# A written sequence for each engine, shared bursts for head pairs, and a last step of plain products

## The chip, the cores and the metric

The kernel runs on one core of a Trainium2 chip. A core has a matrix engine (PE; its weight loads are shown apart as PEld), a vector engine (DVE), a scalar engine with function tables (ACT), a general engine (POOL) and a queue for transfers (SP). Each works through its own instructions in the order in which they were written and waits where it needs another's result. The metric is device microseconds of one execution: 678.94 us, median of 3 runs (678.92 to 679.0).

## The reference

Windowed attention with 8 global tokens and a bias by distance, and behind it a dense layer of 512 to 2048 to 512 with g = h cos(h):

```python
scores = scale * np.matmul(q, k.transpose(0, 1, 3, 2))         # 4 x 8 heads x 768 x 768
is_local = (rel >= 0) & (rel < n_local)                        # n_local 96, n_global 8
scores = np.where(is_global | is_local, scores + bias, -1e9)
a = np.exp(scores - scores.max(-1, keepdims=True)); a /= a.sum(-1, keepdims=True) + 1e-9
x = np.matmul(a, v)                                            # 3072 tokens x 512
h = x @ w_in; out = (h * np.cos(h)) @ w_out
```

## The kernel before

**Attention.** The sequences are cut into 11 parts (`OPEN`, `BLOCKS`): the first batch into two of four blocks of 96 tokens, the others into two of three blocks and one of two. A unit is one part and one pair of heads, 44 in all. For a unit PE writes scores (line 663 or 667), DVE puts masks in and takes the extreme (685, 694), ACT takes exponents with their sums (719), DVE forms reciprocals (727, 730), POOL multiplies (`norm`, 743 and 748), PE turns the result over (847), ACT and DVE bring it to SBUF as `pv`, and a *burst* (890) multiplies it with the values into a bank `px`. The burst's matmuls use 64 columns of the array for each of the two heads, all other large products use 128. `plan_x` splits the bank into a high and a low part (`xmem`).

**Dense layer.** 104 steps (`self.seq`). A step multiplies one or two groups of 128 hidden columns (`m1`, line 973, 12 or 24 matmuls), ACT and DVE form g (991, 994, 997, 1030), g is split into `gh` and `gl`, and after a lag the second product follows. Parts 0 to 2 use plain products (986). From part 3 on (`FAST`) a step of 2 x 2 blocks uses seven products in place of eight (1191), after Strassen and Winograd: DVE or POOL form sums of blocks of g (`sf`, `sh`, `sl`), sums of the weights were stored before (`plan_combined`) and are streamed in (`ws`). Each product is three matmuls of 128x256, high times high, high times low and low times high. Banks A to D collect them over the eight steps of a part, and at a part's end nine additions (`plan_outputs`) give two output tiles; the last part has a version of its own (`plan_last`, 1231). Parts 0 to 2 have a simple copy (`plan_store`, 1262).

**What sets the order.** `Plan` knows each operation with its engines, guessed costs, predecessors and tile classes. `Plan.run` (154) is a list schedule: at each moment a free engine takes, of the operations whose inputs are there by its own clock, the one with the earliest due time, and an operation that several engines may do goes to the one that would end it first, weighted by `HURRY` and `WEIGHT`. Tiles and banks are given out on the way. `emit` writes the result, and until 45 us of the plan's clock it puts matmuls on zeros (`idle`, 1518) into gaps on PE. Only two of the eight banks serve scores, turned tiles and bursts in the later parts (`att`). Two units share a burst where a part has two blocks or its number is in `MERGE`:

```python
MERGE = tuple(range(11, 11))                                   # line 67: none
both = nb == 2 or n in MERGE                                   # plan_values
cls = "part" if keep else "wu" if m < FAST else "oo"           # plan_store
```

Of the kernel before, what the change touches and what calls it, by code (L numbers as in the profile page):

```python
# [10 lines left out]
F32 = mybir.dt.float32  # L11
F32R = mybir.dt.float32r
# [9 lines left out]
P = 128  # L22
# [44 lines left out]
MERGE = tuple(range(11, 11))  # L67
DIFFER = tuple(range(4, 11))
BEFORE = {0: 4000, 1: 2500, 2: 25000}
# [4 lines left out]
FILL_TO, FILL_REST, FILL_EACH, FILL_FIRST, FILL_COLD = 45000, 150, 250, 10, 7000  # L74


class Slot:


    def __init__(self, cls, make):  # L80
        self.cls, self.make = cls, make
        self.users = 0
        self.at = None
        self._tile = None
# [21 lines left out]
class Plan:  # L106
# [7 lines left out]
    AHEAD = 2500  # L114
    SWITCH = 170
    DRAIN = 113
    DEFER = 4000

    def __init__(self, places, free):
        self.ops = []  # L120
        self.places = {c: list(v) for c, v in places.items()}
        self.busy = {}
        self.free = dict(free)
        self.port = 0
        self.mode = None
        self.last = {}

    def drained(self, o, e):

        last = self.last.get(e)  # L130
        return e in (DVE, POOL) and last is not None and (last in o.after or o.apart or last.apart)

    def op(self, engines, emit, after=(), uses=(), due=None, table=None, extra=0, port=False, mode=None):
        o = Op(engines, emit, after, list(uses), due, table, extra, port, mode)
        for a in o.after:
# [6 lines left out]
    def dues(self):  # L142
        late = 10**9
        for o in reversed(self.ops):
            d = late if o.due is None else o.due
            for t in o.then:
                d = min(d, t.due - min(t.engines.values()) - self.WAIT[next(iter(o.engines))] - o.extra)
            o.due = d

    def place(self, u, t):  # L150

        return min(self.places[u.cls], key=lambda p: self.busy.get(p, 0))

    def run(self):

        self.dues()
        for i, o in enumerate(self.ops):
            o.key = (o.due - min(o.engines.values()), i)
        ready = {e: [] for e in self.free}
        coming = []  # L160
        for o in self.ops:
            if o.left == 0:
                for e in o.engines:
                    ready[e].append(o)
        table = "exp"
        out = []
        dma = 0
        t = 0
        inf = 10**12
        todo = len(self.ops)  # L170
        import heapq

        heap = sorted(set(self.free.values()))
        while todo:
            assert heap, [(o.engines, o.key) for e in ready for o in ready[e]][:20]
            t = heapq.heappop(heap)
            while heap and heap[0] == t:
                heapq.heappop(heap)
            again = True
            while again:  # L180
                again = False
                for e, f in self.free.items():
                    if f > t:
                        continue
                    if e == SP and dma - t > self.AHEAD:
                        heapq.heappush(heap, dma - self.AHEAD)
                        continue
                    best = None
                    held = self.port > t
                    holds = lambda o, x: x == POOL or (x == DVE and o.port)  # L190
                    rank = None
                    for o in ready[e]:
                        if o.ready > t:
                            continue
                        key = o.key
                        if self.drained(o, e):
                            key = (key[0] + self.DEFER * (self.last[e] in o.after), key[1])
                        if rank is not None and key >= rank:
                            continue
                        if held and holds(o, e):  # L200
                            continue
                        if len(o.engines) > 1:
                            wait = lambda x: max(t, self.free[x], self.port if holds(o, x) else 0) - t
                            cost = lambda x: wait(x) + o.engines[x] * (HURRY if t < HURRY_TO else WEIGHT)[x]
                            if any(cost(x) < cost(e) for x in o.engines if x != e):
                                continue
                        taken, ok = set(), True
                        for u in o.uses:
                            if u.at is None:
                                p = next(  # L210
                                    (p for p in self.places[u.cls] if self.busy.get(p, 0) <= t and p not in taken),
                                    None,
                                )
                                if p is None:
                                    ok = False
                                    break
                                taken.add(p)
                        if ok:
                            best, rank = o, key
                    if best is None:  # L220
                        continue
                    o = best
                    if e == ACT and o.table and table and o.table != table:
                        same = [x for x in ready[e] if x.table == table and x.ready <= t]
                        if table == "exp" and same:
                            o = min(same, key=lambda x: x.key)
                    for u in o.uses:
                        if u.at is None:
                            u.at, u.begin = self.place(u, t), t
                            self.busy[u.at] = inf  # L230
                    for x in o.engines:
                        ready[x].remove(o)
                    d = o.engines[e]
                    if self.drained(o, e):
                        d += max(0, self.DRAIN - (t - f))
                    self.last[e] = o
                    if e == ACT and o.table and o.table != table:
                        d += self.TABLE
                        table = o.table
                    if e == PE:  # L240
                        if o.mode != self.mode:
                            d += self.SWITCH
                        self.mode = o.mode
                    o.start, o.engine = t, e
                    end = t + d
                    if holds(o, e):
                        self.port = end
                    self.free[e] = end
                    heapq.heappush(heap, end)
                    if e == SP:  # L250
                        dma = max(end + 300, dma) + o.extra
                        end = dma + 1400
                    out.append(o)
                    todo -= 1
                    for u in o.uses:
                        u.users -= 1
                        u.end = max(getattr(u, "end", 0), end + self.WAIT[e] + (SLACK // 2 if u.cls == "att" else 0))
                        if u.users == 0:
                            self.busy[u.at] = u.end
                            heapq.heappush(heap, u.end)  # L260
                    for n in o.then:
                        n.left -= 1
                        n.ready = max(n.ready, end + (self.WAIT[e] + n.slack * (2 if e == POOL else 1) if list(n.engines) != [e] else 0))
                        if n.left == 0:
                            for x in n.engines:
                                ready[x].append(n)
                            heapq.heappush(heap, max(t, n.ready))
                    again = True
        self.length = max(self.free.values())
        return out  # L270


class Net:
# [143 lines left out]
    def plan_weight(self, src, out, at, place, n, due):  # L417

        nc, p = self.nc, self.plan
# [58 lines left out]
    def plan_combined(self, q):  # L478
# [56 lines left out]
        def keep(e):  # L535
            nc.sync.dma_start(self.store(q, 4), f32(self.wo[f, 1]))

        p.op({SP: 470}, keep, done[1], [b], extra=870, due=due)

    def store(self, q, k):  # L540
        if (q, k) not in self.stored:
# [1053 lines left out]
```

## Time and profile before

| | |
|---|---|
| median of 3 runs | 678.94 us |
| span of the profiled execution | 676.7 us |
| outside the span, against the median | 2.2 us |
| PE busy | 663.8 us, 98% of the span |
| DVE, ACT, POOL busy | 554.6, 508.7, 391.0 us |
| useful matmuls end | 669.9 us |
| last output transfer issued | 671.4 us |

The profiled execution's own time is its span and what lies around it; the table sets its span beside the median of the runs. PE's busy time counts zero matmuls and slow changes between kinds of matmul as work, so 98% doesn't mean that nothing is to be had; where the starts of matmuls lie apart tells more. The granted clock of PE stays at its upper level from the first microseconds to the end of the matmuls.

### The profile page before, as it was taken

How to read it: one execution, taken by the hardware profiler on the slowest of the kernel's cores; microseconds unless marked ns; L12 is line 12 of the kernel's file. 1: busy time of each engine (PE TensorE's matmuls, PEld its weight loads, DVE VectorE, ACT ScalarE, POOL GpSimd, SP SyncE). 2: the span in 40 equal slices, each digit the busy share in tenths (PEclk: the TensorE clock that was granted, in tenths of full speed). 3: DMA queues.
4: the chain of work that ended last, by engine and by line, in shares of the span. 5: the costliest groups of instructions: out<-in, count | busy, mean ns of one | idle time of the engine just before them, and what ended most of it. 6: DMA issues, size and time to landing. Idle time of an engine off the chain costs nothing. (4 is left out here: it accounts for less than half of the span.)

```text
span 676.7 us, 17496 instructions
## 1 busy us (share of the span) xinstructions
PE 663.8 (98%) x5810; PEld 626.7 (93%) x5810; DVE 554.6 (82%) x1726; ACT 508.7 (75%) x1253; POOL 391.0 (58%) x576
## 2 busy tenths in 40 slices
PE   8999999999999999999999999999999999999995
PEld 4769999999999998999999999999999999999995
DVE  7999898978898897777778888797878898887664
ACT  7999997579776785866778878676787788684432
POOL 5896544437457553467866776736876768532201
PEclk9999999999999999999999999999999999999999
DMA  8999200044546665877887867787687777665664
GB/s 279 336 321 380 80 1 1 22 159 121 163 139 194 221 183 174 239 220 203 244 240 207 249 213 231 245 239 232 210 240 219 235 228 235 199 224 187 191 226 150
DMA packets 86291, 136.69 MB, mean 202 GB/s; under 512 B 9904, under 2 KB 33968, under 8 KB 86192
## 3 DMA queue, kind: packets, MB, share of 16 engines
q1 hardware_dynamic: 86048, 135.23, 64.7%
q8 instruction: 48, 0.79, 0.5%
q14 instruction: 51, 0.42, 0.2%
q10 hardware_dynamic: 144, 0.26, 0.1%
HBM read 118.67 MB, written 16.78 MB: 200 GB/s over the span
## 5 line engine op out<-in xcount | busy, mean ns | idle before, releaser
L973 PE MATMUL bank<-xmem,w 128*128 128x256 f32 (+1 forms) x2112 | 344.4, 295 | 0.1
L973 PEld LDWEIGHTS bank<-xmem,w 128*128 128x128 f32 x2112 | 294.1, 189 | 7.7 <-issue 0.9
L719 ACT ACTIVATE tt<-tt,st 96x104 f32<-96x104 f32 (+1 forms) x256 | 94.6, 371 | 7.2 <-DVE st L694 6.5
L997 ACT ACTIVATE rr<-rr,half_pi 128x512 f32<-128x512 f32 (+1 forms) x104 | 71.6, 691 | 23.3 <-DVE rr L994 22.1
L986 PE MATMUL bank<-w,gh 128*128 128x256 f32 (+1 forms) x384 | 88.3, 320 | 0.0
L991 ACT ACTIVATE rr<-bank 128x512 int32<-128x512 f32 (+1 forms) x104 | 57.9, 558 | 30.9 <-PE bank L973 29.1
L1191 PE MATMUL bank<-ws,sh 128*128 128x256 f32 x384 | 75.8, 284 | 1.3 <-DVE oo L299 1.3
L994 DVE SCALAR_TENSOR_TENSOR rr<-rr,bank 128x512 f32<-128x512 int32 (+1 forms) x104 | 66.5, 639 | 8.2 <-ACT rr L991 7.6
L784 POOL TENSOR_TENSOR qk<-raw,qk 64x304 fp32r<-64x304 f32 (+1 forms) x57 | 50.0, 880 | 28.4 <-ACT qk L297 6.9
L748 POOL TENSOR_TENSOR tt<-tt,st 96x416 f32<-96x416 f32 (+1 forms) x60 | 45.4, 764 | 35.3 <-DVE sf L1137 9.1
L986 PEld LDWEIGHTS bank<-w,gh 128*128 128x128 f32 x384 | 62.7, 188 | 1.1
L1030 DVE TENSOR_TENSOR rr<-bank,rr 128x512 f32<-128x512 f32 x72 | 49.3, 684 | 16.6 <-ACT rr L997 16.4
L986 PE MATMUL bank<-w,gl 128*128 128x256 f32 (+1 forms) x192 | 61.1, 318 | 0.0
L1191 PEld LDWEIGHTS bank<-ws,sh 128*128 128x128 f32 x384 | 58.6, 188 | 2.0 <-issue 1.4
L297 ACT CAST gh<-rr 128x384 fp32r<-128x384 f32 (+1 forms) x76 | 39.5, 520 | 25.8 <-DVE rr L1030 10.8
L694 DVE CUSTOM_DVE_ANT_0 tt<-bank,dd 96x104 f32<-96x104 f32 (+1 forms) x256 | 55.0, 256 | 2.2
L1191 PE MATMUL bank<-ws,sl 128*128 128x256 f32 x192 | 54.1, 282 | 0.1
L997 ACT ACT_TABLE_LOAD x40 | 51.3, 1283 | 0.7
L719 ACT ACT_TABLE_LOAD x39 | 50.0, 1283 | 0.7
L445 POOL TENSOR_SCALAR raw<-raw 128x512 bf16<-128x512 bf16 (+1 forms) x32 | 36.6, 1167 | 23.6 <-DVE w L466 13.2
L667 PE MATMUL bank<-qk 128*96 128x200 f32 (+1 forms) x384 | 49.1, 257 | 0.0
L1191 PE MATMUL bank<-w,gh 128*128 128x256 f32 x256 | 48.7, 282 | 0.0
(137 smaller groups left out, 1532.4 us busy)
## 6 DMA issues: line engine op xcount, KB each, us to landing
ws<-sum SPq DMA_DIRECT2D x256, 256.0 KB
raw<-in_qk_dram SPq DMA_DIRECT2D x48, 174.0 KB
raw<-in_w_in_dram SPq DMA_DIRECT2D x16, 512.0 KB
sum<-sw SPq DMA_DIRECT2D x64, 128.0 KB
raw<-in_qk_dram SPq DMA_DIRECT2D x48, 150.0 KB
raw<-in_qk_dram SPq DMA_DIRECT2D x48, 148.0 KB
out_dram<-oo SPq DMA_DIRECT2D x23, 256.0 KB
raw<-in_w_out_dram SPq DMA_DIRECT2D x16, 256.0 KB
```

What stands on the lines that cost most here:

```text
L667: nc.tensor.matmul(out, qs[:, m, q0], ks[:, k : k + w], start=m == 0, stop=m == 1)
L694: nc.vector.tensor_tensor_reduce(tt[t // 2].tile[:, t % 2, j, :w], ps.tile[:R, i * WIN : i * WIN + w], self.dd[:, v, :w], op0=ALU.add, op1 ...
L719: nc.scalar.activation(x, x, AF.Exp, bias=st.tile[:, c : c + 1], scale=-1.0, accum_out=st.tile[:, n2 + c : n2 + c + 1])
L748: self.eng(e).tensor_tensor(x, x, r.broadcast_to([R, na, SLOT]), op=ALU.mult)
L784: self.eng(e).tensor_tensor(ks[D:, k0:k1], raw.tile[D:, k0:k1], ks.bitcast(F32)[D:, k0:k1], op=ALU.subtract)
L973: self.nc.tensor.matmul(ph, self.wi[f][:, w, kk * P : (kk + 1) * P], xx[:, kk, :], start=kk == 0 and m == 0, stop=kk == self.NK - 1 and m ...
L986: self.nc.tensor.matmul(out, gg, w[:, i, :], start=start and m == 0 and h == 0, stop=stop and m == 2)
L991: self.nc.scalar.activation(r.bitcast(I32), ph, AF.Copy, scale=1.0 / TWO_PI, bias=0.25)
L994: self.nc.vector.scalar_tensor_tensor(r, r.bitcast(I32), -TWO_PI, ph, op0=ALU.mult, op1=ALU.add)
L997: self.nc.scalar.activation(r, r, AF.Sin, bias=self.half_pi)
L1030: {DVE: dve(512)}, lambda e: nc.vector.tensor_tensor(r(), h(), r(), op=ALU.mult), [o], [ph, rr],
L1191: nc.tensor.matmul(out, x, y, start=q == 0 and j == 0 and half == 0, stop=q == self.NF // 2 - 1 and j == 2 and ends)
```

## The change

A table `ORDER` gives each operation its place in one common sequence and its engine (t PE, a ACT, d DVE, g POOL, s SP). `Plan.run` follows it and only hands out tiles and banks; due times, costs and weights choose nothing any more. `MERGE` holds parts 2 to 10, so that the three-block parts too have two units in a burst. In the last step (`plan_last`) the seven products become eight plain ones of three matmuls, in two banks `att` and one `ph` that start empty; the additions for the seven steps before are done with `plan_outputs`, and what the eight products give is added to the result. Its `g` is split over its full 512 columns, its block sums go. `plan_store` of part 2 uses tiles `oo`. Two thresholds of the zero matmuls move. `COPIED`, `APART` and `BEHIND` are empty and change nothing; `low` in `step` is 0 wherever `step` runs.

```diff
-MERGE = tuple(range(11, 11))
+MERGE = tuple(range(2, 11))
-FILL_TO, FILL_REST, FILL_EACH, FILL_FIRST, FILL_COLD = 45000, 150, 250, 10, 7000
+FILL_TO, FILL_REST, FILL_EACH, FILL_FIRST, FILL_COLD = 52000, 250, 250, 10, 7000
+ORDER = {
+    "": "1s 0d 2d 3d 4d 5d 7d 8d 13d 14d",
+    "v0.0": "10s 55s",
...
 class Plan:
+    def ordered(self):
+        at, out = {}, [None] * len(self.ops)
+        names = dict(t=PE, a=ACT, d=DVE, g=POOL, s=SP)
+        for o in self.ops:
+            part = o.name.split(" ")[0]
+            i = at[part] = at.get(part, -1) + 1
+            rank = self.table(part)[i]
+            o.engine = names[rank[-1]]
+            out[int(rank[:-1])] = o
+        return out
     def run(self):
-        self.dues()
-        ready = {e: [] for e in self.free}
...
+        out = self.ordered()
+        for o in out:
+            for u in o.uses:
+                if u.at is None:
+                    free = [p for p in self.places[u.cls] if p not in held and p not in taken]
+                    u.at = min(free, key=lambda p: clear.get(p, 0))
...
 def plan_step
-        c0 = HALF if fast else 0
+        c0 = HALF if fast and s < len(self.seq) - 1 else 0
 def plan_fast
+        if s == len(self.seq) - 1:
+            self.plan_last(s, m, q, self.po, gg, g, self.before, due)
+            return
 def plan_last
+        (one, *first), (two, *second) = self.plan_outputs(m, po, last, due, False)
+        X, Y, Z = self.bank(), self.bank(), self.bank("ph")
+        plan = (
+            (1, X, lo, 0, 0, two, second), (2, X, hi, 0, 1, two, second), (3, Y, lo, 1, 0, one, first), (4, Z, hi, 1, 1, one, first),
+        )
+        for i, b, half, t, c, _, _ in plan:
+            for k in range(2):
+                def times(e, i=i, b=b, half=half, t=t, c=c, k=k):
+                    (ah, al), (bh, bl) = left(k, t), (row(c) if k else top[c])()
+                    for j, (x, y) in enumerate(((ah, bh), (ah, bl), (al, bh))):
+                        nc.tensor.matmul(half(b), x, y, start=i != 2 and k == j == 0, stop=i != 1 and k == 1 and j == 2)
+        for i, b, half, t, c, out, before in plan[1:]:
+            done[i] = p.op({DVE: 420 if i > 2 else 685}, step, [*before, ends[i]], [b, out], due=due)
 def plan_store
-            cls = "part" if keep else "wu" if m < FAST else "oo"
+            cls = "part" if keep else "wu" if m < FAST - 1 else "oo"
```

How the sequence changes is seen at three places. First PE at the first attention of part 2, before (pv, v: the burst; qk: scores of the next unit; xmem: `m1`; gh, gl: second products), two cuts from before:

```order
L973 MATMUL bank<-xmem,w 128x384 x3
L890 MATMUL bank<-pv,v 64x96 x10
L667 MATMUL bank<-qk 96x96 x2
...
L986 MATMUL bank<-w,gl 128x512
L973 MATMUL bank<-xmem,w 128x384 x3
L890 MATMUL bank<-pv,v 64x96 x10
```

and the same two units now:

```order
L1439 MATMUL bank<-ident,tt 96x96 x2
L1439 MATMUL bank<-ident,tt 104x96 x4
L1573 MATMUL bank<-xmem,w 128x384 x12
L1490 MATMUL bank<-pv,v 64x96 x20
L1255 MATMUL bank<-qk 96x96 x2
```

Two bursts of ten products have become one of twenty. Over the program PE has 38 bursts before and 26 now.

Second ACT and DVE where part 2 ends and part 3 starts (`oo<-bank` is the copy that empties a bank; the numbers tell tiles apart). ACT before, and behind the dots DVE before:

```order
L997 ACTIVATE rr_3977<-rr_3977,half_pi_112 128x512
L297 COPY oo_4019<-bank_3134 128x512
L991 ACTIVATE rr_4050<-bank_3980 128x512
...
L994 SCALAR_TENSOR_TENSOR rr_4050<-rr_4050,bank_3980 128x512
L299 COPY oo_4070<-bank_3151 128x512
L1030 TENSOR_TENSOR rr_4050<-bank_3980,rr_4050 128x512
```

and ACT now:

```order
L883 CAST gh_4029<-rr_3964 128x384
L883 COPY oo_4032<-bank_3220 128x512
L883 COPY oo_4048<-bank_3213 128x512
L1591 ACTIVATE rr_4062<-bank_3977 128x512
```

Both copies stand on ACT, one behind the other, and go to the two tiles `oo0` and `oo1`; before, both went to the one tile `late1`.

Third DVE at the end of the program, before:

```order
L1041 TENSOR_TENSOR gl<-rr,gh 128x384
L1137 TENSOR_TENSOR sf<-rr,sf 128x128
L1144 TENSOR_TENSOR sl<-sf,sh 128x512
L1242 TENSOR_TENSOR oo<-oo,bank 128x256
L1242 TENSOR_TENSOR mid<-mid,bank 128x256
L1242 TENSOR_TENSOR oo<-mid,oo 128x256
```

and now:

```order
L1630 TENSOR_TENSOR rr<-bank,rr 128x512
L885 CAST gh<-rr 128x512
L1815 TENSOR_TENSOR oo<-oo,bank 128x256 x3
L1815 TENSOR_TENSOR oo<-oo 128x256 x2
L1815 TENSOR_TENSOR oo<-oo,bank 128x256 x2
L1870 TENSOR_TENSOR oo<-oo,bank 128x512
L1870 TENSOR_TENSOR oo<-oo,bank 128x256 x2
```

The sums of blocks are gone, `gl` of the last step is POOL's last instruction, and three additions are left behind the last products.

The counts by engine change too. DVE takes from POOL 33 instructions of `norm` (9 of 96x416, 16 of 96x208, 8 of 96x192; it had none), 20 low parts of keys (64x304), 8 differences of values and most of the sums of blocks; it has 12 casts `sh` (none before), 16 more casts `gh`, and 25 sign operations on weights (8 before). `raw<-raw,steep` (the first units' queries) stands 2 times on ACT (7 before), 5 on POOL (1) and once on DVE. ACT has 8 fewer loads of a function table, PE 39 zero matmuls (48).

## Rows read from the trace of the kernel before

**Rows 1.** Page, part 1 (busy us, share, instructions) and the clock by slices.
```profile
PE 663.8 (98%) x5810; PEld 626.7 (93%) x5810; DVE 554.6 (82%) x1726; ACT 508.7 (75%) x1253; POOL 391.0 (58%) x576
...
PEclk9999999999999999999999999999999999999999
```

**Rows 2.** Windows: length, busy us by engine, clock, DMA share, GB/s.
```profile
10.00:60.00 50.00, 48.18 (x475) 35.52 (x473) 46.44 (x218) 49.71 (x169) 41.78 (x50) 1.00 0.99 340
60.00:100.00 40.00, 40.00 (x261) 37.61 (x261) 35.74 (x62) 40.00 (x90) 19.98 (x20) 1.00 0.32 108
100.00:170.00 70.00, 69.99 (x480) 65.74 (x479) 59.91 (x164) 54.60 (x128) 35.35 (x50) 1.00 0.24 75
170.00:260.00 90.00, 90.00 (x779) 84.03 (x778) 81.36 (x252) 70.68 (x172) 49.34 (x64) 1.00 0.58 183
260.00:340.00 80.00, 77.64 (x710) 75.46 (x709) 58.29 (x183) 55.08 (x131) 48.80 (x77) 1.00 0.74 215
340.00:620.00 280.00, 279.95 (x2650) 274.70 (x2650) 231.82 (x736) 213.78 (x519) 182.28 (x271) 1.00 0.75 226
```

**Rows 3.** Waits of PE from 60 us on: total us, times, longest.
```profile
PE bank L1191 <- DVE oo L299: 1.3, 1, 1.3
PE bank L847 <- DVE pv L299: 0.7, 1, 0.7
```

**Rows 4.** Zero matmuls: timeline of the first and second run of them, group by form.
```profile
1.05 3.91 PE L1518 MATMUL idle<-zeros 128*128 128x512 bf16 x10 [1.05 <-DVE zeros L307]
...
8.49 3.41 PE L1518 MATMUL idle<-zeros 128*128 128x512 bf16 x15
...
L1518 PE MATMUL idle<-zeros 128*128 128x512 bf16 x48 | 13.7, 420 | 1.1 <-DVE zeros L307 1.1
```

**Rows 5.** Timeline of PE around one burst: start us, us, instruction.
```profile
257.12 0.88 PE L973 MATMUL bank<-xmem,w 128*128 128x256 f32 x6
257.93 0.39 PE L890 MATMUL bank<-pv,v 104*64 104x96 f32 x4
258.15 0.34 PE L890 MATMUL bank<-pv,vd 96*64 96x96 f32 x4
...
259.15 0.33 PE L890 MATMUL bank<-pv,vd 96*64 96x96 f32 x4
259.42 0.97 PE L973 MATMUL bank<-xmem,w 128*128 128x256 f32 x6
```

**Rows 6.** Tile oo, 255 to 275 us: its instruction, what ended idle time.
```profile
L299 DVE COPY oo<-bank x1: 691/691/691, 269.3 to 269.3; 128x512 f32<-128x512 f32 x1
its engine sat idle before it (us, times) until:
  DMA out_dram<-oo: 1.9, 1
```

**Rows 7.** Timeline of the end.
```profile
662.06 0.40 PE L1191 MATMUL bank<-w,gh 128*128 128x256 f32 x2
...
664.44 0.69 DVE L1030 TENSOR_TENSOR rr<-bank,rr 128x512 f32<-128x512 f32 x1 [0.79 <-ACT rr L997]
...
664.53 0.40 PE L1191 MATMUL bank<-w,gh 128*128 128x256 f32 x2
...
668.12 0.19 PEld L1191 LDWEIGHTS bank<-ws,sl 128*128 128x128 f32 x1 [0.25 <-DVE sl L1144]
...
669.63 0.28 PE L1191 MATMUL bank<-ws,gl 128*128 128x256 f32 x1
...
670.76 0.42 DVE L1242 TENSOR_TENSOR oo<-mid,bank 128x256 f32<-128x256 f32 x1
...
671.41 0.38 ACTq L1258 DMA_DIRECT2D out_dram<-oo  x1
```

**Rows 8.** Groups by form: busy us, mean ns; and line 1144's spread, min/median/max.
```profile
L618 ACT ACTIVATE raw<-raw,steep 128x384 f32<-128x384 f32 x7 | 4.3, 615 | 3.7 <-POOL small L357 2.8 <-DMA raw<-in_qo_dram 0.8
...
L442 DVE TENSOR_SCALAR raw<-raw 128x512 uint16<-128x512 uint16 x8 | 6.4, 796 | 0.0
...
L1144 DVE TENSOR_TENSOR sl<-sf,sh x41: 647/693/1409, 261.5 to 667.4; 128x512 fp32r<-128x512 f32 x41
L1144 POOL TENSOR_TENSOR sl<-sf,sh x23: 1277/1289/1300, 291.8 to 637.3; 128x512 fp32r<-128x512 f32 x23
```

More of the change, by code (lines that the diff above doesn't have):

```diff
@@ new lines, with measured @@
+FILL_TO, FILL_REST, FILL_EACH, FILL_FIRST, FILL_COLD = 52000, 250, 250, 10, 7000
+def measured(e, part, name, d):
+    if e == PE:
+        if name == "score":
+            return {278: 350}.get(d, d - 2 if d < 400 else d)
+        return {"m1": {348: 358}, "times": {348: 355}, "turn": {340: 300, 170: 128}, "m2": {700: 702}}.get(name, {}).get(
+            d, d * 168 // 160 if name == "burst" else d)
+    if e == ACT:
+        if name in ("wbias", "wlow"):
+            return d + 12 if d < 400 else d - 12
+        if part[0] == "s" and name in ("op1", "op3"):
+            return d + (10 if name == "op1" else 16)
+        return d + {"khigh": 36, "qhigh": 16}.get(name, 0)
+    if e == DVE:
+        if name == "wsign":
+            return d * 83 // 100
+        return {120: 100}.get(d, d + 2 if d > 100 else d)
+    if e == POOL:
+        if name == "wsign":
+            return d * 89 // 100
+        if name == "wlow":
+            return d + (130 if d < 500 else 50)
+        if name == "wrest":
+            return d + 50 if d < 1000 else d
+        more = dict(krest=33, khigh=19, low=33, step=33, norm=15, op13=35, op15=35, wbias=40, whigh=40, queries=60)
+        return d + more.get(name, 8)
+    return d
@@ L121, in __init__ @@
         self.places = {c: list(v) for c, v in places.items()}
-        self.busy = {}
         self.free = dict(free)
[L124 to L131, printed above, removed]
-    def op(self, engines, emit, after=(), uses=(), due=None, table=None, extra=0, port=False, mode=None):
+        self.part, self.count, self.tables = "", {}, {}
+    def op(self, engines, emit, after=(), uses=(), due=None, table=None, extra=0, port=False, mode=None):
+        name = emit.__name__
+        if name == "<lambda>":
+            self.count[self.part] = self.count.get(self.part, 0) + 1
+            name = f"op{self.count[self.part]}"
+        engines = {e: measured(e, self.part, name, d) for e, d in engines.items()}
         o = Op(engines, emit, after, list(uses), due, table, extra, port, mode)
+        o.name = f"{self.part} {name}"
         for a in o.after:
@@ L140, in op @@
         return o
[L142 to L152, printed above, removed]
-    def run(self):
-        self.dues()
-        for i, o in enumerate(self.ops):
-            o.key = (o.due - min(o.engines.values()), i)
-        ready = {e: [] for e in self.free}
[L160 to L268, printed above, removed]
@@ new lines, in run @@
+    def run(self):
+        out = self.ordered()
+        port, dma, mode, table = 0, 0, None, "exp"
+        last, held, clear = {}, set(), {}
+        for o in out:
+            e = o.engine
+            taken = []
+            for u in o.uses:
+                if u.at is None:
+                    free = [p for p in self.places[u.cls] if p not in held and p not in taken]
+                    u.at = min(free, key=lambda p: clear.get(p, 0))
+                    taken.append(u.at)
+            held.update(taken)
+            t = self.free[e]
+            for a in o.after:
+                t = max(t, a.end + (self.WAIT[a.engine] if list(o.engines) != [a.engine] else 0))
+            for u in o.uses:
+                if u.begin is None:
+                    t = max(t, clear.get(u.at, 0))
+            holds = e == POOL or (e == DVE and o.port)
+            if holds:
+                t = max(t, port)
+            for u in o.uses:
+                if u.begin is None:
+                    u.begin = t
+            d = o.engines[e]
+            x = last.get(e)
+            if e in (DVE, POOL) and x is not None and (o.apart or x.apart or x in o.after):
+                d += max(0, self.DRAIN - (t - self.free[e]))
+            last[e] = o
+            if e == ACT and o.table and o.table != table:
+                d += self.TABLE
+                table = o.table
+            if e == PE:
+                if o.mode != mode:
+                    d += self.SWITCH
+                mode = o.mode
+            o.start = t
+            end = self.free[e] = t + d
+            if holds:
+                port = end
+            if e == SP:
+                dma = max(end + 300, dma) + o.extra
+                end = dma + self.LAND
+            o.end = end
+            for u in o.uses:
+                u.users -= 1
+                u.end = max(u.end, end + self.WAIT[e])
+                if u.users == 0:
+                    held.discard(u.at)
+                    clear[u.at] = u.end
@@ L489, in plan_combined @@
         one, two, tops = make(), make(), (make(), make())
-        done = [[x] + self.prev.get("sums", []) for x in done]
+        done = [[x] + self.prev.get("sums", self.joined[BEHIND:] if BEHIND else []) for x in done]
         view = lambda s: f32(s.tile)
@@ L1225, in plan_outputs @@
         v3 = p.op(ps, ad(c21, c21, bank(lo, D)), [v4, last["D"]], [D, two], due=due)
+        if not store:
+            return (one, v1, v2), (two, v3, v4)
         for z, t, after in ((one, 1, [v1, v2]), (two, 0, [v3, v4])):
@@ new lines, in plan_last @@
+        done = {}
+        for i, b, half, t, c, out, before in plan[1:]:
+            part = half if i > 2 else lambda x: x.tile
+            step = lambda e, b=b, out=out, part=part: self.eng(e).tensor_tensor(part(out), part(out), part(b), op=ALU.add)
+            done[i] = p.op({DVE: 420 if i > 2 else 685}, step, [*before, ends[i]], [b, out], due=due)
+        for x, t, after, e, queue, cs in (
+            (two, 0, [done[2]], SP, nc.sync, slice(0, 512)),
+            (one, 1, [done[3]], ACT, nc.scalar, slice(0, MW)),
+            (one, 1, [done[4]], SP, nc.sync, slice(MW, 512)),
+        ):
```

584 lines of the change are left out of this document (530 added, 54 removed), and 152 rows, old and new, of the table ORDER.

## The prediction

> **What bounds the kernel now.** I read the page's engine line and clock first: PE is busy for 98% of the span and its granted clock is full, 2.4 GHz, in every slice [rows 1]. Then the windows, for where PE is not busy: from 60 to 260 us and from 340 to 620 us it idles 0.06 us in all, from 260 to 340 us 2.36 us, and from 10 to 60 us 1.8 us [rows 2]. Then PE's waits, which name two in the middle: 1.3 us for a copy by DVE and 0.7 us for another [rows 3]. A busy PE hides two things that only the timeline shows. Of 48 zero matmuls (13.7 us busy) ten run before the first scores, in 3.9 us, and cost nothing; the other 38 take 9.8 us, 0.26 us each, and stand where PE had nothing to do [rows 4]. And a change from one kind of matmul to another is counted as work. So PE sets the time from about 60 us on, and behind it only three things can give time: fewer or cheaper PE instructions, an earlier full PE, and a shorter end. Beside PE, ACT is full from 10 to 100 us (89.7 of 90 us) and DVE is busy for 93% of 10 to 60 us [rows 2]: the ramp belongs to them.
>
> The sum is made against the profiled execution (span 676.7 us); the median of the runs lies 2.2 us above it, and I carry that over.
>
> **Shared bursts.** Twelve bursts fewer, with the same products. What a burst costs beyond its products is read at one: six matmuls start at 257.12 and the burst at 257.93, where six at the pitch of 0.118 us (21 matmuls from 662.06 to 664.53, [rows 7]) take 0.71, so 0.10 goes to the change; its eight groups lie 0.167 apart (258.15 to 259.15 is six of them) but the first took 0.22, another 0.05; and from the last group to the next `m1` are 0.27 where 0.17 would do, 0.10 [rows 5]. Together 0.25 us, times 12: -3.0 us. It is on PE in stretches where PE is full, so it counts whole if the rest keeps up. Bounds: -3.0, and 0 where PE waits instead (a rival below).
>
> **The sequence in the middle.** The 1.3 us wait is PE's first product of part 3, for a bank that DVE emptied at 269.3, and DVE had itself waited 1.9 us for an output transfer, since its copy was to go to the tile that the transfer before was still reading [rows 3, 6]. Now both copies go to two tiles and stand on ACT, behind one another. That wait goes: -1.3. The 0.7 us wait and the rest (2.36 in all from 260 to 340) come from the old order; a new order may have others, so I take half of the rest, -0.5. Sum -1.8; bounds -2.4 (all gone) and +1.5 (one wait like the 1.3 new).
>
> **The ramp.** ACT loses five multiplications of queries at 0.615 us, 3.1 us [rows 8], in a stretch in which it has 0.3 us idle out of 50 [rows 2]; up to the eighth second product the order gives it otherwise about the same work. POOL and DVE take them over, and DVE has 3.6 us idle there and gets two or three us more. The zero matmuls, which stand for the planned gaps, are 29 behind the first ten in place of 38: 9 times 0.26 is 2.3 us. So -3.1 by ACT and -2.3 by the gaps if DVE follows, about -1 if DVE's room is what counts. I take -2.0, bounds -5 (half of the 9.8 us of zeros gone) and +1. SP's transfers change places too, with DMA at 0.99 of its time from 10 to 60 us [rows 2]; none of PE's early waits is for one, and the bytes are the same, so I price that at 0 inside these bounds.
>
> **The end.** The last product of h and cos(h) ends at 664.44 + 0.69 = 665.13 [rows 7]. Behind it now come a cast of 128x512 on DVE (no row has it; about 0.4, between nothing and ACT's like at 0.6), and `gl` on POOL, for which the nearest row is POOL's subtraction of 128x512 with 1.29 [rows 8]; with 0.1 for each of two handovers, 667.0. PE's fourteen older products from 662.06, 2.47 per seven, end at 667.0 too. So the eight products start without a wait; 24 matmuls at 0.118 put the last start at 669.7, against 669.63 now [rows 7]: one product more (+0.35) is paid by the stall for `sl`, 0.25 with a weight load behind it at 668.12, which goes with the sums. What goes besides is the tail of additions: the last matmul's start lies 1.78 before the last transfer's issue at 671.41 now; then it needs its own 0.28, a handover of 0.1, one addition of 0.42 and an issue, 0.85. So -0.9. The older additions (nine) run beside the eight products. The halved last transfer may land sooner, which no row prices. Bounds -1.3 and +0.4 (POOL's `gl` 1.3 late).
>
> **Sum.** -3.0 - 1.8 - 2.0 - 0.9 = -7.7: span 669.0, with 2.2 us around it 671.2 us.
>
> **The load on DVE.** The order moves work from POOL, where an instruction takes about twice as long (1.29 against 0.69 us for `sl`, [rows 8]), to DVE. Kind by kind, with the rows' means where a row has the form, DVE gets about 20 us more up to the `m1` that runs at 169 us before; the largest kind is eight sign operations at 0.796, 6.4 us [rows 8]. This is an estimate. From 10 to 170 us DVE had 17.9 us idle [rows 2]. I take it as hidden, since the durations hold waits (`sl` on DVE takes 0.647 at the least and 1.409 at the most, [rows 8]) and POOL, with some 70 us less to do, should block less; the sum has no term for it.
> The Trainium skill, "SBUF — State Buffer", section "Who interferes with whom", says that a DVE instruction with two inputs in SBUF and a POOL instruction that reads SBUF shut each other out for a whole instruction. The spread of `sl` agrees. By that rule the added 20 us would shrink and the first rival below loses chance; without it I would give that rival more.
>
> **Rivals.**
> *DVE becomes the bound until 170 us* (slower). For it: the 20 us. It decides at how full DVE can get: PE has no idle there, so each us that DVE is short goes to PE. The other terms give -5.7 (the ramp's is lost). At 97% busy DVE has room for 155.2 - 142.1 = 13.1, is short by 6.9, and the result is +1.2, 680.1 us; at 93%, as in the ramp, it is short by 13 and the result 686. Break-even is 97.8%. Against it: shorter blocked instructions, and that some of the added work is only earlier. Chance 0.13.
> *The shared burst waits for banks.* Two units' `px` fill both `att` banks at once, and until ACT and DVE have split them neither scores nor turned tiles can be written. If PE ran dry for 0.5 us behind each of 12, 6 us of the gains go: 677.2 with everything else, 678.5 if the ramp gives 1 less. Against it: the order puts 12 or more `m1` matmuls (1.4 us) behind most shared bursts. Chance 0.08.
> *The order only trades waits.* Bursts and end stay, middle and ramp give nothing: -3.9, 675.0. Chance 0.14.
> *The ramp gives all its zeros can.* -5 in place of -2, all middle waits gone: 667.6, and below that if PE's full stretch starts even sooner. Chance 0.12.
> *The clock falls.* Fewer zero matmuls leave bare gaps. Ten took 3.91 at the start, 0.39 each, and fifteen 3.41 later, 0.23 each [rows 4]: a stretch of 4 us at the lower level, 1.2 GHz, costs some 2 us. One such stretch gives 673.2, inside my own range. Chance 0.03.
> The Trainium skill, "TensorE: Matmul & The Clock Gate", has the clock fall when the array idles; here it stays full over gaps of up to 1.3 us, so the rule changes only this small chance.
>
> **How the numbers follow.** The forecast, all four terms with their sizes within about two us, has 0.50: 668 to 675. With the rivals it makes 0.50 + 0.14 + 0.12 + 0.03 and a quarter of the bank rival faster by more than 0.2% (1.4 us, about what a measurement of this kernel can tell), 0.81; half of the bank rival and a little of the first, 0.06, within it; 0.13 slower. The range from 666 to 680 leaves out what lies past the first rival's price at 97% (about 0.09) and a ramp better than -6 (0.06).
>
> **What would show it.** Right: from 60 to 620 us PE idle below 0.5 us, 26 bursts; no wait of PE for `oo` at a part's end; the `m1` that runs at 169 us some 3 us earlier; last transfer issued within 1.0 us of the last matmul's start. Wrong: PE waits for DVE (`pv`, `xmem`, or weights) between 60 and 200 us, with DVE at 97% and more; PE idle behind shared bursts; a clock below full before 660 us.

## The result and the profile after

The changed kernel took 682.45 us (median of 4 runs, 681.92 to 683.37) against 678.93 us for the kernel before beside it: a ratio of 1.0056, 95% interval 1.0042 to 1.0070. It is 3.5 us slower, and the forecast was 7.7 us faster. The profiled execution has a span of 680.5 us (676.7 before).

The page's engine line and clock (the slices, in tenths), which answer to [rows 1]:

```profile
PE 662.0 (97%) x5804; PEld 626.0 (92%) x5804; DVE 584.2 (86%) x1866; ACT 482.2 (71%) x1218; POOL 323.5 (48%) x459
...
PEclk9999999999999999999999999999999999999999
```

The clock is full throughout. DVE has 30 us more and POOL 67 us less. The same stretches as in [rows 2] (length, busy us of PE, PEld, DVE, ACT, POOL, clock, DMA share, GB/s):

```profile
10.00:60.00 50.00, 47.31 (x470) 35.49 (x468) 48.65 (x225) 48.42 (x166) 36.47 (x46) 1.00 1.03 322
60.00:100.00 40.00, 39.83 (x259) 37.20 (x258) 38.10 (x74) 37.08 (x78) 8.84 (x12) 1.00 0.43 132
100.00:170.00 70.00, 69.46 (x477) 65.10 (x475) 64.78 (x186) 55.85 (x133) 27.49 (x34) 1.00 0.27 82
170.00:260.00 90.00, 89.96 (x785) 84.63 (x784) 79.57 (x247) 63.12 (x163) 51.77 (x59) 1.00 0.55 169
260.00:340.00 80.00, 79.75 (x729) 78.63 (x728) 72.26 (x243) 58.49 (x148) 35.20 (x55) 1.00 0.79 236
340.00:620.00 280.00, 272.40 (x2592) 266.31 (x2591) 237.57 (x776) 198.54 (x491) 139.70 (x194) 1.00 0.73 220
```

From 340 to 620 us PE idles 7.60 us where it idled 0.05 us. The stretch from 260 to 340 us, with the 1.3 us wait that was to go, did improve: 0.25 us in place of 2.36. PE's waits from 60 us on (total us, times, longest), which answer to [rows 3]:

```profile
PE bank L1439 <- POOL tt L1340: 3.4, 5, 1.5
PE bank L1255 <- DVE qk L1366: 1.0, 2, 0.7
PE bank L1786 <- POOL sl L1747: 0.9, 1, 0.9
PE bank L1573 <- DVE rr L1630: 0.8, 2, 0.4
PE bank L1786 <- POOL sh L887: 0.7, 1, 0.7
PE bank L1439 <- DVE st L1282: 0.5, 1, 0.5
```

The copies at part 2's end are not among them. No single tile is to blame: it is `norm`, low keys, sums of blocks, and `rr`. The longest of these waits can be followed through the timeline of all engines (start us, us, instruction, idle time before it and what ended that):

```profile
555.73 1.28 ACT L1597 ACT_TABLE_LOAD   x1
...
555.95 0.19 DVE L1318 RECIPROCAL st<-st 96x6 f32<-96x6 f32 x1
...
557.02 0.84 POOL L1376 TENSOR_TENSOR qk<-raw,qk 64x304 fp32r<-64x304 f32 x1 [0.59 <-DVE qk L1376]
557.03 0.73 ACT L1597 ACTIVATE rr<-rr,half_pi 128x512 f32<-128x512 f32 x1
...
557.65 0.58 ACT L1591 ACTIVATE rr<-bank 128x512 int32<-128x512 f32 x1
...
558.13 0.31 ACT L883 COPY pv<-bank 104x192 f32<-104x192 f32 x1
...
558.47 0.82 DVE L1456 TENSOR_TENSOR pv<-bank,own 96x192 f32<-96x192 f32 x2 [1.54 <-ACT pv L883]
...
558.88 0.28 PE L1786 MATMUL bank<-w,sl 128*128 128x256 f32 x1
559.21 0.36 DVE L1340 TENSOR_TENSOR tt<-tt,st 96x208 f32<-96x208 f32 x1
...
559.74 0.88 POOL L1340 TENSOR_TENSOR tt<-tt,st 96x416 f32<-96x416 f32 x1 [1.88 <-DVE tt L1340]
...
560.67 0.70 PE L1439 MATMUL bank<-ident,tt 96*104 96x96 f32 x6 [1.52 <-POOL tt L1340]
```

Read it from the bottom. PE wants to turn the tile that POOL normalises. All that POOL needs was there at 556.14, when the reciprocal ended, but POOL starts at 559.74. Until 557.86 it is held by the low part of keys that stands ahead in its own queue; the 1.88 us after that it waits for DVE's `norm` of another tile, since the program makes a POOL instruction wait for the DVE instruction that stands ahead of it in the common sequence and is marked `port` in the code (mostly those with two inputs in SBUF). DVE is late because its multiplication `own` waits 1.54 us for ACT's copy out of the same bank, and ACT had a table load, a cosine and an angle in front of that copy, 2.5 us from the load's start to the angle's end. Four engines' queues (PE, POOL, DVE, ACT) stand in one chain, with no room in any of them.

Line 1456 shows the middle link over the whole program (DVE's `own`, and what ended the idle time of DVE before it; in the kernel before it was 2.9 us in 8 places):

```profile
L1456 DVE TENSOR_TENSOR pv<-bank,own x76: 339/354/554, 12.2 to 608.8; 96x192 f32<-96x192 f32 x40, 96x384 f32<-96x384 f32 x36
its engine sat idle before it (us, times) until:
  ACT pv L883: 5.4, 5
```

Of the 33 turned tiles that ACT copies and DVE multiplies, not one is read by both at once. The Trainium skill, "PSUM — Partial Sum Buffer", section "PSUM bank collisions raise a hardware error", says that two engines must not touch the same partitions of one bank at once, reads against reads included, and that software has to keep them apart. Here the program does, with 0 of 33 overlapping, in the kernel before too; what an overlap would do, no run here shows.

**Where the time went.** I took the start of each matmul to the start of the next, less the usual pitch of its kind, and summed it by cause (us against the kernel before; the last column is the sixth experiment below):

| term | forecast | changed kernel | order with reserve |
|---|---|---|---|
| bursts | -3.0 | -2.8 | -2.8 |
| ramp: zero matmuls and waits until 60 us | -2.0 | -1.1 | -1.8 |
| waits from 60 to 640 us | -1.8 | +8.7 | -0.7 |
| end: one product more, stall for `sl`, tail | -0.9 | -0.5 | -0.7 |
| sum | -7.7 | +4.3 | -6.0 |
| span | -7.7 | +3.8 | -6.2 |

What is left between sum and span, 0.5 and 0.2 us, isn't traced to a place; small differences of pitch can make it. The 8.7 us are 12.4 us of waits now less 3.7 us before. They are more than the idle time of the windows, since the end that the trace gives for a 128x256 matmul lies 0.16 us past the point at which the next one could start (0.28 long, 0.118 apart), so each wait behind one costs that much more than the idle time shown.

### The profile page after: what moved, and what is told of

The parts are those of the page before. It is cut to its first block, busy times and chain, and to the rows that moved or that the text cites. A ratio compares the mean times of both kernels' runs of the same rounds, so it can differ in the third digit from the quotient of the medians.

```text
span 680.5 us, 17313 instructions
## 1 busy us (share of the span) xinstructions
PE 662.0 (97%) x5804; PEld 626.0 (92%) x5804; DVE 584.2 (86%) x1866; ACT 482.2 (71%) x1218; POOL 323.5 (48%) x459
## 4 chain that ended last, share of the span: by engine, by line
## 5 line engine op out<-in xcount | busy, mean ns | idle before, releaser
L1573 PE MATMUL bank<-xmem,w 128*128 128x256 f32 (+1 forms) x2112 | 304.5, 295 | 1.6 <-DVE rr L1630 0.8
L1573 PEld LDWEIGHTS bank<-xmem,w 128*128 128x128 f32 x2112 | 279.7, 188 | 7.6 <-DVE rr L1696 1.8
L1586 PE MATMUL bank<-w,gh 128*128 128x256 f32 (+1 forms) x384 | 86.4, 318 | 0.0
L1786 PE MATMUL bank<-ws,sh 128*128 128x256 f32 x378 | 71.2, 281 | 0.8 <-POOL sh L887 0.7
L1282 DVE CUSTOM_DVE_ANT_0 tt<-bank,dd 96x104 f32<-96x104 f32 (+1 forms) x256 | 57.9, 257 | 3.5
L1340 POOL TENSOR_TENSOR tt<-tt,st 96x416 f32<-96x416 f32 (+1 forms) x43 | 34.3, 804 | 53.0 <-DVE st L1318 12.6
L1376 POOL TENSOR_TENSOR qk<-raw,qk 64x304 fp32r<-64x304 f32 (+1 forms) x41 | 39.9, 975 | 31.0 <-PE bank L1439 5.0
L1255 PE MATMUL bank<-qk 128*96 128x200 f32 (+1 forms) x384 | 47.6, 256 | 1.2 <-DVE qk L1366 1.0
L1307 ACT ACTIVATION_READ_ACCUMULATOR tt<-tt,st 96x1 f32 x256 | 48.4, 189 | 0.0
L1255 PEld LDWEIGHTS bank<-qk 128*96 128x96 f32 x384 | 41.8, 162 | 3.1 <-DVE qk L1366 1.3
```

The source lines that it names most:

```text
L1255: nc.tensor.matmul(out, qs[:, m, q0], ks[:, k : k + w], start=m == 0, stop=m == 1)
L1282: nc.vector.tensor_tensor_reduce(tt[t // 2].tile[:, t % 2, j, :w], ps.tile[:R, i * WIN : i * WIN + w], self.dd[:, v, :w], op0=ALU.add, op1 ...
L1307: nc.scalar.activation(x, x, AF.Exp, bias=st.tile[:, c : c + 1], scale=-1.0, accum_out=st.tile[:, n2 + c : n2 + c + 1])
L1340: self.eng(e).tensor_tensor(x, x, r.broadcast_to([R, na, SLOT]), op=ALU.mult)
L1376: self.eng(e).tensor_tensor(ks[D:, k0:k1], raw.tile[D:, k0:k1], ks.bitcast(F32)[D:, k0:k1], op=ALU.subtract)
L1573: self.nc.tensor.matmul(ph, self.wi[f][:, w, kk * P : (kk + 1) * P], xx[:, kk, :], start=kk == 0 and m == 0, stop=kk == self.NK - 1 and m ...
```

## The experiments

All are timed against the kernel before on the same chip (medians 677.75 to 678.26 us there). A ratio is worked out from all the runs and can lie 0.1% off the ratio of the medians, 0.7 us in experiment 6. Each trace is of one execution, and executions of one kernel spread: by 4.6 us in 5, whose traced one was its slowest (680.61 us). Two theories stood against each other. **Theory A:** the written sequence leaves no reserve between what another engine brings and PE's use of it, so each small delay reaches PE; the other parts give what was forecast. **Theory B:** two units in a burst bunch the attention's work, and no order helps. Each recorded expectation states which theories it sets against each other; in 3 and 4 the letters A and B stand for other theories than these two.

**1. The three other parts under the old list schedule** (no table):

```diff
-MERGE = tuple(range(11, 11))
+MERGE = tuple(range(2, 11))
...
+            self.plan_last(s, m, q, self.po, gg, g, self.before, due)   # eight plain products
...
-            cls = "part" if keep else "wu" if m < FAST else "oo"
+            cls = "part" if keep else "wu" if m < FAST - 1 else "oo"
```

> The kernel before with its own list schedule, and with the three other parts of the change: shared bursts in parts 2 to 10, the last step of eight plain products, part 2's copies in two tiles. Theory 1 (the written sequence is what costs; the other parts give what the traces show of them, 2.7 us at the bursts and 0.7 us at the end): 673.5 to 676.5 us, that is 2.5 to 5.5 us below the kernel before. Theory 2 (the shared bursts or the new last step starve PE, whatever the sequence): 681 us or more, with PE idle between 340 and 620 us of 5 us and more. A new list schedule may add or take about 1.5 us either way.

681.7 us against 677.75, ratio 1.0060 (1.0043 to 1.0077). Theory 1's number failed, and with it the idea that the table alone costs the time. Theory 2's time came, with less idle time than its 5 us: the bursts gave their 2.9 us, but PE idles 3.35 us from 340 to 620 us, in a traced execution that at 679.2 us was the fastest of the four:

```profile
340.00:620.00 280.00, 276.65 (x2628) 270.67 (x2628) 232.96 (x747) 202.05 (x495) 165.79 (x240) 1.00 0.74 223
```

**2. Shared bursts alone, list schedule** (`MERGE` as above and nothing else).

> The kernel before with its own list schedule and one edit: two units share a burst in parts 2 to 10 too. Theory 1 (a shared burst saves the change of kind, 0.22 us each, and costs nothing): 676.3 us, 2.6 us below before, within 1.5 us for the new schedule. Theory 2 (a shared burst makes PE wait for banks): same or slower than before, 679 to 683 us, with PE idle behind bursts.

680.0 us, ratio 1.0041 (1.0026 to 1.0056). Its window and its longest waits:

```profile
340.00:620.00 280.00, 276.87 (x2641) 271.90 (x2640) 233.45 (x745) 199.07 (x499) 166.38 (x240) 1.00 0.74 223
```

```profile
PE bank L973 <- DVE rr L1030: 2.3, 4, 0.6
PE bank L667 <- DVE qk L774: 1.0, 1, 1.0
PE bank L667 <- DVE st L694: 0.8, 2, 0.5
```

3.13 us idle in place of 0.05. The waits are not behind the bursts and not for the split of `px`, as the rival on shared bursts had it, but for keys, `rr` and extremes some microseconds away from them. So under this schedule sharing brings waits. Both theories could still explain it.

**3. POOL no longer waits for the DVE instruction ahead of it.**

```diff
-                    self.tc.add_manual_dep(new[0], held_by.name, behind, reason="port")
+                    pass
```

> The changed kernel with one line less: a POOL instruction no longer waits for the DVE instruction of two inputs that stands ahead of it in the common sequence, where it needs nothing of it. Theory A (POOL's norm comes late because it queues behind a DVE that is itself late): the 4.8 us that PE waits for POOL's norm go for the greater part, 677 to 680 us. Theory B (that order only replaces a lockout that the two engines give each other anyway): DVE's and POOL's instructions get longer in its place, 681 to 686 us.

695.37 us, ratio 1.0266 (1.0245 to 1.0286), 14 us worse than the changed kernel by the two ratios and past the range of either theory, on the side of the second. The page's engine line, to set beside that of the changed kernel (same instructions on the same engines):

```profile
PE 667.6 (96%) x5804; PEld 627.9 (91%) x5804; DVE 607.4 (88%) x1866; ACT 482.6 (70%) x1218; POOL 343.5 (50%) x459
```

DVE's instructions got 23 us longer, POOL's 20 us. One group by form of this kernel, the low parts of keys on DVE (busy us, mean ns), whose mean was 541 ns in the changed kernel:

```profile
L1376 DVE TENSOR_TENSOR qk<-raw,qk 64x304 fp32r<-64x304 f32 x20 | 14.3, 723 | 0.9 <-POOL qk L887 0.4
```

PE's waits for POOL's `norm` did fall (4.8 to 1.1 us), and others took their place. So the wait that stood in the longest chain protects more than it costs. The Trainium skill, "SBUF — State Buffer", section "Who interferes with whom", says that a DVE instruction with two inputs in SBUF contends with a POOL instruction that reads SBUF, for ports that are an exclusive lock. The trace agrees as far as instructions of both engines got longer, 541 to 723 ns on DVE in the group above; the lock itself no row shows.

**4. `norm` back on POOL** (25 letters in the table, as here in unit 9.3):

```diff
-    "u9.3": "... 4135g 4121d 3983d 4136t ..."
+    "u9.3": "... 4135g 4121g 3983d 4136t ..."
```

> The changed kernel with its sequence, but all 25 norm operations that it has on DVE (33 instructions, some 10 us) are on POOL again, as before. Theory A (DVE is too full, and what queues on it comes late): less to do for DVE, 678 to 681 us. Theory B (POOL is slower at the same instruction, 0.9 us against 0.4 us, and the sequence leaves it no room): PE waits for POOL's norm more often, 683 to 690 us.

683.75 us, ratio 1.0090 (1.0074 to 1.0107). The second theory's number. Less work for DVE did not help here, but that doesn't clear DVE: the places in the sequence stayed while the same `norm` takes longer on POOL (683 against 366 ns for 96x208 and 876 against 615 ns for 96x416 at line 1340 of the changed kernel; the 0.9 against 0.4 us of the expectation mixes these shapes). What clears it is 6, which keeps all of DVE's work and has almost no waits.

**5. Same instructions, same engines, room for one wait.** The table's ranks are rearranged so that, by the plan's prices, nothing is late when the two readers of a turned tile come one after the other.

> The changed kernel with the same instructions on the same engines, and another order: the table's ranks are moved so that none of PE's work is late when DVE and ACT read one turned tile one after the other. In the trace of the changed kernel the two never read it at once (0 of 33 pairs overlap, and DVE waits 5.4 us for ACT's copies there), while the table has places that only fit if they do. Theory A (that one wait, which the sequence leaves no room for, is behind about half of PE's 10.9 us of waits between 60 and 640 us): 5 to 6 us less than the changed kernel, so 1 to 3 us below the kernel before; the waits at the places where the other causes act stay. Theory B (two units in a burst bunch the work of the attention, whatever the order): within 1.5 us of the changed kernel, 2 to 5 us above the kernel before.

677.27 us, ratio 0.9990 (0.9980 to 1.0000): about 4.5 us less than the changed kernel and 0.7 below before. PE's idle time from 340 to 620 us is 3.91 us in place of 7.60:

```profile
340.00:620.00 280.00, 276.09 (x2623) 270.04 (x2622) 238.38 (x779) 200.76 (x495) 143.29 (x198) 1.00 0.75 220
```

That is just short of what theory A expects (5 to 6 less, 1 to 3 below before), and outside theory B's 1.5 us. Since the whole order moved (4685 of its 4872 places), this doesn't prove that the one wait alone made the difference.

**6. Same instructions, same engines, with a reserve.** The ranks are arranged as in 5, and also so that PE has 0.3 us (0.6 us behind POOL) between another engine's result and its use. Against the changed kernel 4693 of 4872 places move and no engine changes. At the place of the long wait:

```diff
-    "u9.3": "... 4101d 4102d 4135g 4121d 3983d 4136t ..."
+    "u9.3": "... 4100d 4101d 4102g 4115d 3978d 4132t ..."
```

The numbers are places in the common sequence, the letters engines. POOL's `norm` (4135g) stood one place ahead of PE's turn (4136t) and behind DVE's `norm` of the other tile; now it follows the reciprocal (4101d) at once, 30 places ahead of the turn.

> As the run before, but ordered so that there is also a reserve of about 0.3 us (0.6 us behind POOL) between what another engine brings and PE's use of it. Same instructions, same engines. Theory A (the sequence had no reserve; the rest of the change gives what was forecast for it): the waits go almost all, 9 to 11 us less than the changed kernel, 4 to 7 us below the kernel before. Theory B (bunching by shared bursts): within 2 us of the changed kernel.

672.09 us against 677.99, ratio 0.9902 (0.9885 to 0.9918): 5.9 us faster than the kernel before, and 10 us better than the changed kernel by the two ratios. Two of its windows, its waits of PE from 60 us on, and what its `own` waits for:

```profile
260.00:340.00 80.00, 79.19 (x724) 78.00 (x722) 70.44 (x238) 58.38 (x146) 36.35 (x57) 1.00 0.80 231
340.00:620.00 280.00, 279.52 (x2669) 275.76 (x2668) 241.84 (x789) 201.53 (x494) 141.22 (x200) 1.00 0.75 226
```

```profile
PE bank L887 <- POOL qk L1008: 0.7, 1, 0.7
PE bank L1205 <- DVE rr L1262: 0.4, 1, 0.4
PE bank L887 <- DVE xmem L1170: 0.4, 1, 0.4
PE bank L1205 <- DVE rr L1328: 0.2, 1, 0.2
```

```profile
its engine sat idle before it (us, times) until:
  PE bank L1071: 1.1, 2
  ACT pv L515: 0.7, 2
```

0.48 us idle from 340 to 620 us, and from 60 us on no wait for `norm` at all, with the same bursts, the same engines and DVE 2% busier there. Theory A holds, and theory B as "no order helps" falls.

**7. Last step and tile copies, list schedule, no sharing** (the second and third part of the diff of 1).

> The kernel before with its own list schedule, with the last step of eight plain products and part 2's copies in two tiles, and without shared bursts in the parts of three blocks. Forecast's own terms (0.7 to 0.9 us at the end, 1.3 us for the wait that went): 1.5 to 2.5 us below the kernel before if the new list schedule is as good as the old. Rival (a list schedule made anew after any edit brings waits of its own, of 1 to 3 us, which is what the run of all three parts showed): 0 to 2 us above the kernel before.

677.65 us, ratio 0.9996 (0.9986 to 1.0005): no gain, as the rival had it, at the lower edge of its 0 to 2 us. From 60 to 340 us PE idles 0.02 us in place of 2.37, but 1.70 us from 340 to 620. So this new list schedule took in one stretch what it gave in another.

**8. Shared bursts, list schedule, its reserve raised** (`MERGE` as in 1, `SLACK` 450 in place of 350).

> The kernel before with its list schedule, shared bursts in parts 2 to 10, and the reserve that the list schedule keeps ahead of PE's attention work raised from 350 to 450 ns. With 350 ns it was 2.3 us above the kernel before. Theory A (the loss there was a reserve too small for the tighter attention): at or below the kernel before. Theory B (bunching): 1.5 us or more above it again.

680.35 us, ratio 1.0037 (1.0026 to 1.0048): B's number. The wider reserve of the list schedule, which it keeps only ahead of the attention's own steps, didn't help the time (PE's idle time from 340 to 620 us is 1.71 us in the traced execution, 3.13 in that of 2); 6 shows that the cause is not in the sharing as such.

**9 and 10. No sharing in the parts of three blocks, in an order with reserve,** with the list schedule's engines (9) and with engines chosen anew (10); the last step and the tiles are the changed kernel's.

The table is another one throughout; the diff shows the only other line.

```diff
-MERGE = tuple(range(2, 11))
+MERGE = tuple(range(11, 11))
...
```

> The changed kernel without shared bursts in the parts of three blocks (12 bursts more), with the engines that the list schedule of the kernel before chooses, and in an order with the reserve of the run that was 5.9 us below before. Theory F (a shared burst is worth what the traces show of it, 0.22 us each, and no more): 2.7 us above that run, 2 to 4 us below the kernel before. Theory B (sharing costs waits that take most of its gain, which the list schedules seemed to show): at that run's time or below, 5 us or more below the kernel before. Theory C (that run's gain is the new order's alone, and would come to any set of instructions): also 5 us or more below; what tells it from B is PE's waits, which B puts near zero here and C as in that run.

> As the run before, but with engines chosen anew as well (93 instructions more on DVE, 70 fewer on POOL, as the change does). Against the run before it shows what the change's move of work from POOL to DVE is worth where the order has a reserve: 0 to 1.5 us less by the forecast, which gave it no term of its own; more than 2 us would say that the placement matters in itself. Against the run with sharing it shows the sharing alone: 2.7 us more.

9: 677.51 us against 678.26, ratio 0.9989 (0.9973 to 1.0005). 10: 675.78 us, ratio 0.9959 (0.9946 to 0.9971). Nine came out 2.4 us slower than F's number (2.7 above experiment 6, which is 3.2 below before) and far from B and C. So a reserve by itself doesn't give 5.9 us to any set of instructions; the changed set was needed. From 9 to 10, the choice of engines gives 1.7 us by the medians, just above the expected 0 to 1.5; from 10 to 6, sharing gives 3.7 us by the same.

**11. Like 6, with some instructions on other engines** (28 more on DVE, 20 fewer on POOL, 8 fewer on ACT; in all 360 of the 4872 entries name another engine, where the expectation says some 40).

> The changed kernel in an order with reserve, as in the run that was 5.9 us below before, with some 40 instructions on other engines too (28 more on DVE). If that run's time is what the reserve gives and not luck of one order: 5 to 7 us below the kernel before again. If single orders scatter as the list schedules did: anywhere from 3 us below to 1 us above.

674.06 us, ratio 0.9944 (0.9927 to 0.9961): 4.2 us below before, short of the 5 to 7. Single orders scatter by some 2 us even with the reserve, unless the engines make the difference: PE idles 2.01 us from 340 to 620 us here. Against this run, sharing is worth 1.7 us, against 6 it is 3.7; the 2.8 us of the traces lie between.

Over all orders from a table, PE's idle time from 340 to 620 us is 0.48, 0.96, 0.31 and 2.01 us in the four with a reserve (6, 9, 10, 11), and 7.60 and 3.91 us in the two without (the changed kernel and 5). So the written order is shown to be the cause; that it is its missing reserve rests on these six orders.

## Why the prediction was wrong

The step that failed is "The sequence in the middle": "Sum -1.8; bounds -2.4 (all gone) and +1.5 (one wait like the 1.3 new)." It measured +8.7. The part of it that rests on rows was right: the wait for part 2's copies went, and 260 to 340 us got 2.1 us better. The upper bound was not: I took the new order's unknown waits to be at most one like the one that I saw. Nothing in the trace of before says so. That trace had PE idle 0.05 us from 340 to 620 us under a schedule which kept a reserve, and I read this as a property of the work and not of the schedule. The sign was in the code: the old `run` adds `SLACK` of 350 ns ahead of the attention's work on PE, twice that behind POOL, and half of it when a bank comes free; the new one uses none of these. By its own prices the table leaves PE 0.13 us of waits after 60 us; on the chip they were 12.4, of which 15 places made 10.9. The plan's own waits don't tell a good order from a bad one either: by the same prices the orders of 5, 6, 9, 10 and 11 have 0.01 us at the most. A plan that fits to the last tenth has no answer to what it doesn't know, such as one bank's two readers.

Point by point:
- **Bursts:** -3.0 forecast, -2.8 measured, 0.23 us each. In the changed kernel this was paid away by waits, but not as the rival "the shared burst waits for banks" put it (0.08): PE didn't run dry behind the bursts. The result was on that rival's side for another reason.
- **Ramp:** -2.0 forecast, -1.1 measured: 1.4 us fewer zero matmuls and 0.3 us more waits. The term was right in kind and too large; 1.8 came in experiment 6. DVE is 97% busy from 10 to 60 us (48.65 of 50), but that isn't shown to be the reason: in 6 it is 98% busy (49.19).
- **End:** -0.9 forecast, -0.5 measured. The cast took 0.43 us (0.4 assumed), `gl` 1.30 (1.29), and the eight products started without a wait. From the last product's start to the span's end are 6.3 us in place of 7.0.
- **DVE becomes the bound until 170 us** (0.13): fell. DVE was busy for 102.9 of the 110 us from 60 to 170 us and PE idled 0.71 us there. It had the right sign and the wrong place.
- **The order only trades waits** (0.14): nearest in name, but it allowed no more than as many waits as before.
- **The load on DVE:** taken as hidden, with no term of its own. In 6 it is, with the same work on DVE.
- **A slip in a sum:** the bank rival's second price, 678.5, comes out of its own terms at 678.2; it changes no chance and not the range.
- **Clock:** full, as said.

With an order that has a reserve, the four terms come out at -2.8, -1.8, -0.7 and -0.7, and the time 5.9 us below before, against 7.7 forecast. So the sum was that of a kernel which the change could have been.

What stays open: how much of the 10.9 us belongs to each cause (two readers of a bank, lockouts between POOL and DVE, late transfers) isn't separated, since 5 moved the whole order. Nor is it settled why the list schedule loses with shared bursts even at a larger reserve. Part of it is planned: by its own prices the schedule of 2 has PE wait 4.1 us after 60 us and that of 8 3.9, against 1.5 before.

## What to carry to other kernels

When an order is replaced, ask what margin the old one kept and whether the new one keeps it: a full engine in the trace says that the old schedule was good, not that the work is easy to schedule. Bound the cost of a new order by the places at which the full engine uses a result soon after it comes, not by the waits that the old trace shows. And follow a long wait back through all the queues before taking out its last link: the POOL wait that seemed to cost 4.8 us was worth 14.

## What the runs showed of the hardware

- Without an order between DVE instructions of two inputs and POOL's, the same instructions took 23 us more on DVE and 20 us more on POOL, and the kernel 14 us more (experiment 3).
- A burst of 64-column matmuls among full ones costs 0.23 us beyond its products (2.8 us over 12, the changed kernel against the one before).
- In this program a wait of PE behind a 128x256 product costs 0.16 us more than the idle time that the windows show (0.28 us long, 0.118 apart).
